# A planner's rules replaced by tables: the order on all engines of a gated mix of attention and feed-forward

## The chip, the cores and the metric

The kernel runs on one core of a Trainium2 chip. The metric is the device time of one execution in microseconds, as the median of several runs. The engines are named as the profile names them: PE (TensorE, the matmuls), DVE (VectorE), ACT (ScalarE), POOL (GpSimd) and SP (SyncE, which issues most DMAs).

## The reference

Two branches read the same x (2048 tokens, 512 features) and are mixed per token by a gate. Branch A is attention with a compressive memory: 32 heads of 16 features, four segments of 512 tokens, causal softmax inside a segment, plus a linear-attention read of the memory that earlier segments left. Branch B is a gated feed-forward with 1792 hidden features.

```python
for s in range(4):                                   # segments of 512 tokens
    logits = einsum('bhqd,bhkd->bhqk', qs, ks) * scale + mask
    a_dot = einsum('bhqk,bhkd->bhqd', softmax(logits), vs)
    a_mem = (phi(qs) @ M) / (phi(qs) @ z + 1e-06)
    o = sigmoid(beta) * a_mem + (1 - sigmoid(beta)) * a_dot
    M = M + phi(ks)^T vs;  z = z + sum(phi(ks))
a = concat(o) @ wo
b = (relu(x @ W_gate) * (x @ W_up)) @ W_down
out = g * a + (1 - g) * b            # g = sigmoid(sum(x * gate_w))
```

phi(t) is t + 1 for t > 0 and exp(t) otherwise. All inputs and the output are bfloat16.

## The kernel before

**The work.** For each segment s there are these kinds of work. `proj(s)`: q, k and v by dense matmuls of 128 x 128 on 512 columns (L791, L793), evacuated from PSUM by DVE or ACT (`qcp`, `kcp`, `vcp`), and two masked copies of k (`kmask`, L810 and L811). `att(s)`: the scores in 18 *visits* (`quad`, L913). A visit is a group of matmuls in row tiles of 32 that fills 2048 columns of PSUM, that is four banks; one exponential on ACT (`exp`, L929) turns them into E in SBUF, and POOL masks the diagonal blocks (`mask`, L935). `pv` (L969) multiplies E with V for eight heads at once in two banks, DVE transposes the result (L979) and a chain on DVE and POOL divides, scales and transposes it into oT. `mu` (L836) updates the memory and `num` (L856) reads it. `ffn(s)`: 14 blocks of gate and up matmuls (`wg`, `wu`, L1043), relu on DVE or ACT (L1052, L1051) and a product on DVE (`hm`, L1054). `outp(s)`: per 128 tokens one PSUM bank that sums the down projection (L1082) and the attention's output projection (L1075); DVE or ACT scales it (`fin`, L1091, L1092), and SP stores it. The last 128 tokens are done in a piece of 384 columns and one of 128.

**The start.** Eleven matmuls on constants (`warm`, L693) run while x and the weights land. Sixteen identity matmuls (`xt`, L707) transpose the first segment's x, which is loaded into hT; DVE and ACT copy the pieces to xT. The first q projection (`q0`) goes by quarters of the contraction, one matmul at a time, through four banks, then k, then v. Weights come in quarters (wq, wk, wv: 128 KB each) and in halves of quarters (wg, wu: 224 KB each), all issued by SP in the order wq, wk, wv, wg, wu. x of later segments, k for the memory update (`kT2`) and the memory's output (`aT`) are transposed by DMA, also from SP.

**The order.** Nothing is ordered by the text of the program. Each piece of work is an `Op` with its engines, a duration from a small cost model, and the buffers that it reads and writes. `program` puts the ops into queues with priorities, and `Sched.run` places them one by one: `_choose` takes, for the engine that is free first, the head of the queue that is ready and has the best priority, with random offsets from a list of seeds, one for every 8 us of planned time; `ready` holds back work whose reader is not due, `low` and `visit_in` keep banks free for the next visit, and `_bank_choice` picks PSUM banks. Where an op may run on two engines, the one that can start first gets it. From the placed order each engine's instruction list with its semaphore waits is written out (`_waits`, `emit`), so the chip sees a fixed order, and only waits decide when things run.

**Banks.** Visits always stand on banks 0 to 3:

```python
eps = [Epoch("main", 4, 0)] + [Epoch("side") for _ in range(4, nb)]
```

so a visit cannot start before the exponential of the visit before it is done. Banks 4 to 7 go round among the projections, the feed-forward, pv, mu, num and the output; these may also use low banks when no visit is near.

Of the kernel before, what the change touches and what calls it, by code (L numbers as in the profile page):

```python
# [2 lines left out]

# [6 lines left out]
ALU = mybir.AluOpType  # L10
# [4 lines left out]
LAT = 60.0  # L15
MU_G = 1
LAG = 0
PAIR = 1
LASTK = 17
HWAIT = 250.0  # L20
HEARLY = 3500.0
MWAIT = 500.0
PVR = 2
NEXT = 1150.0
TNN = 2
STRICT = 6000.0
PE_LAT = 175.0
SWITCH = 106.0
GATE_T = {0: 20000.0, 1: 44000.0, 2: 90000.0, 3: 140000.0}
UNIT_T = 400.0  # L30
X1_T = 19000.0
X2_T = 34000.0
H1_T = 14000.0
# [5 lines left out]
SBX = 0  # L39
LOW_T = {"main": 0.0, "att": 3000.0, "proj": 2000.0, "ffn": 2000.0, "mid": 3000.0, "out": 5000.0}  # L40
WIN = 8000.0
EVAC_P = 0.5
ND_P = 0.2
ADP = 1
TSP = 0
OAP = 0
UNITS = [[8] * 18] * 4
ORDER = [[(0, 1, 7, 2, 6, 3, 5, 4), (4, 0, 1, 7, 2, 6, 3, 5)] * 2] * 4
# [30 lines left out]
class Epoch:  # L79
    _n = 0  # L80

    def __init__(self, cls="mid", nb=1, at=None):
        self.nb = nb
        self.at = at
        self.group = (self,)
        Epoch._n += 1
        self.res = f"ACCep{Epoch._n}"
        self.bank = None
        self.readers = []
        self.cls = cls  # L90


class Op:
    __slots__ = ("engs", "eng", "fns", "occs", "lat", "reads", "writes", "name", "dma", "nbytes", "mode", "ep", "role",
                 "after", "nbk", "port", "base", "preds", "stream", "idx", "start", "end", "done", "cidx", "gate", "nd", "mates")

    def __init__(self, alts, reads=(), writes=(), name="", lat=0.0, dma=False, nbytes=0, mode="f", ep=None, role=None):
# [13 lines left out]
        self.after = 0.0  # L111
        self.nbk = 2
        self.port = name.startswith(PORT)
        self.base = None
        self.preds = []
        self.gate = None
        self.mates = ()
# [11 lines left out]
class Sched:  # L129
    ENGS = ("pe", "act", "dve", "pool", "sp")  # L130
    CAPS = {"ffn": 3, "proj": 2, "mid": 2, "out": 2}

    def __init__(self, ndma=16, nbanks=8, seeds=(0,)):
        self.seeds = seeds
        self.jit = {}
        self.knobs = {}
        self.low_from = False
        self.mates = ()
# [9 lines left out]
        self.queues = {e: [] for e in self.ENGS}  # L148
        self.dma_rr = 0
        self.port_free = 0.0  # L150
        self.relax = False
# [7 lines left out]
        self.busy = {e: 0.0 for e in self.ENGS}  # L159
        self.ops = []  # L160
        self.log = []
# [8 lines left out]
    def add(self, op):  # L170
# [42 lines left out]
        self.ops.append(op)  # L213
        return op

    def queue(self, prio, ops):
        by = {}
        for t in ops:
            for e in t.engs:
                by.setdefault(e, []).append(t)  # L220
        for e, ts in by.items():
            self.queues[e].append([prio, ts, 0])

    def _bank_free(self, prev, e):
        if prev is None:
            return 0.0
        return max((r.end + LAT for r in prev.readers if self.know[e][r.stream] < r.idx), default=0.0)

    def pv_due(self):
        q = self.queues["pe"][self.pvq]  # L230
        while q[2] < len(q[1]) and q[1][q[2]].done:
            q[2] += 1
        if q[2] >= len(q[1]) or q[1][q[2]].gate is None:
            return 0
        t = self.now["pe"] + 500.0
        return (PVR if q[1][q[2]].mates else q[1][q[2]].nbk) if all(p.done and p.end <= t for p, _ in q[1][q[2]].preds) else 0

    def next_visit(self):
        q = self.queues["pe"][self.attq]
        while q[2] < len(q[1]) and q[1][q[2]].done:  # L240
            q[2] += 1
        return q[1][q[2]] if q[2] < len(q[1]) else None

    def visit_in(self, dt):
        op = self.next_visit()
        if op is None:
            return False
        t = self.now["pe"] + dt
        if op.after > t or not all(p.done and p.end <= t for p, _ in op.preds):
            return False  # L250
        return all(p.done and p.end <= t + 700.0 for g in op.ep.group for rd in g.readers for p, _ in rd.preds if p.ep not in op.ep.group and p.cidx < op.cidx)

    def soon(self, dt):
        op = self.next_visit()
        if op is None or op.after - HEARLY > self.now["pe"] + dt:
            return False
        if not all(p.done and p.end + LAT <= self.now["pe"] + dt for p, _ in op.preds):
            return False
        t = max((self._bank_free(x, "pe") if x is None or all(r.done for r in x.readers) else 1e9) for x in self.bank_ep[:4])
        return t <= self.now["pe"] + dt  # L260

    def next_sides(self):
        op = self.next_visit()
        return 0 if op is None else len(op.ep.group) - 1

    def low(self, cls):
        return 0 if self.low_from and (self.relax or not self.visit_in(LOW_T[cls])) else 4

    def _bank_choice(self, ep, e, taken=()):
        cls, nb, n = ep.cls, ep.nb, len(self.bank_ep)  # L270
        idle = [i not in taken and (p is None or all(r.done for r in p.readers)) for i, p in enumerate(self.bank_ep)]
        if ep.at is not None:
            own = range(ep.at, ep.at + nb)
            return (ep.at, max(self._bank_free(self.bank_ep[i], e) for i in own)) if all(idle[i] for i in own) else None
        lo = 4 if cls == "side" else self.low(cls)
        if cls in ("proj", "ffn", "mid", "out"):
            held = sum(not f and p.cls == cls for f, p in zip(idle, self.bank_ep))
            if held + nb > (self.knob()[3] if cls == "ffn" else 2):
                return None
            free = sum(idle[lo:])  # L280
            if (free - nb < max(self.pv_due(), 1) if nb == 1 else free < (2 if self.relax else 3)):
                return None
            room = sum(idle[4:]) - (self.next_sides() if self.visit_in(self.knob()[1]) and not self.relax else 0)
        else:
            room = 8
        best = None
        for bi in range(lo, n - nb + 1):
            if not all(idle[bi:bi + nb]) or bi + nb > 4 and min(nb, bi + nb - 4) > room:
                continue
            ft = max(self._bank_free(p, e) for p in self.bank_ep[bi:bi + nb])  # L290
            key = ft + (300.0 if bi < 4 else 0.0)
            if nb == 1:
                key += 0.0 if not idle[bi ^ 1] else 200.0
            if best is None or key < best[2]:
                best = (bi, ft, key)
        return best and best[:2]

    def _banks(self, op, e):
        taken, out, t = set(), [], 0.0
        for ep in op.ep.group:  # L300
            bc = self._bank_choice(ep, e, taken)
            if bc is None:
                return None
            out.append((ep, bc[0]))
            taken |= set(range(bc[0], bc[0] + ep.nb))
            t = max(t, bc[1])
        return out, t

    def _pred_done(self, op, e):
        for p, war in op.preds:  # L310
            if war and not p.dma and p.eng == e and e == "pe" and p.done:
                continue
            yield p

    def ready(self, op, e):
        t0 = self.now[e]
        t = op.after - (HEARLY if op.mode == "r" and self.mode == "h" else 0.0)
        if op.gate is not None:
            if self.mode != "r" and not self.relax and not (op.gate.done and self.now["pe"] > op.gate.start + STRICT) and not (op.gate.done and (self.next_visit() is None or self.soon(NEXT))):
                return None  # L320
            for m in op.mates:
                for p in self._pred_done(m, e):
                    if p.eng != "pe":
                        if not p.done:
                            return None
                        t = max(t, p.end + LAT - 900.0)
            lo = self.low("att")
            ft = sorted(self._bank_free(p, e) for p in self.bank_ep[lo:] if p is None or all(r.done for r in p.readers))
            if len(ft) < op.nbk:
                return None  # L330
            t = max(t, ft[op.nbk - 1])
        for p in self._pred_done(op, e):
            if not p.done:
                return None
            if self.know[e][p.stream] < p.idx:
                t = max(t, p.end + LAT)
        if op.ep is not None:
            if op.role == "w" and op.ep.bank is None:
                for rd in [x for g in op.ep.group for x in g.readers]:
                    for p, _ in rd.preds:  # L340
                        if p.ep in op.ep.group or p.cidx > op.cidx:
                            continue
                        if not p.done:
                            return None
# [858 lines left out]
```

## Time and profile before

| | |
|---|---|
| runs, us | 265.08, 264.30, 264.28 |
| median, us | 264.3 |
| span of the profiled execution, us | 262.7 |
| between the span and the median, us | 1.6 |
| PE busy, us (share of the span) | 255.7 (97%) |
| ACT, DVE, POOL busy, us | 184.5, 179.1, 131.0 |
| granted PE clock | 1.00 |
| DMA, MB moved | 19.87 |

The page gives the span, from the first instruction to the last, and not the device time of the profiled execution itself; the median of the runs stands for that. A line of the page's groups names source line, engine, operation, and output and inputs, then the count, the busy time and the mean duration, and then how long the engine stood idle before and what ended that. A line of a timeline gives the start, the length and the group.

### The profile page before, as it was taken

How to read it: one execution, taken by the hardware profiler on the slowest of the kernel's cores; microseconds unless marked ns; L12 is line 12 of the kernel's file. 1: busy time of each engine (PE TensorE's matmuls, PEld its weight loads, DVE VectorE, ACT ScalarE, POOL GpSimd, SP SyncE). 2: the span in 40 equal slices, each digit the busy share in tenths (PEclk: the TensorE clock that was granted, in tenths of full speed). 3: DMA queues.
4: the chain of work that ended last, by engine and by line, in shares of the span. 5: the costliest groups of instructions: out<-in, count | busy, mean ns of one | idle time of the engine just before them, and what ended most of it. 6: DMA issues, size and time to landing. Idle time of an engine off the chain costs nothing.

```text
span 262.7 us, 6432 instructions
## 1 busy us (share of the span) xinstructions
PE 255.7 (97%) x2619; PEld 114.6 (44%) x2653; DVE 179.1 (68%) x356; ACT 184.5 (70%) x160; POOL 131.0 (50%) x295
## 2 busy tenths in 40 slices
PE   8999999999999999999999999999999999999996
PEld 5444443444443544334444544443444444344444
DVE  5488878789986587778788676757667716477600
ACT  4586689999789779785768787677777665676021
POOL 3036557564646466666555457836365354545100
PEclk9999999999999999999999999999999999999999
DMA  6989646930261134213040242010131101000011
GB/s 197 286 302 281 138 66 148 274 44 22 68 155 25 24 81 117 48 22 33 10 107 13 59 91 23 4 40 2 31 76 40 22 24 34 26 2 2 0 42 40
DMA packets 34925, 19.87 MB, mean 76 GB/s; under 512 B 24016, under 2 KB 34128, under 8 KB 34896
## 3 DMA queue, kind: packets, MB, share of 16 engines
q1 hardware_dynamic: 34800, 19.46, 30.4%
q8 instruction: 21, 0.34, 0.6%
q14 instruction: 8, 0.07, 0.1%
q10 hardware_dynamic: 96, 0.00, 0.0%
HBM read 10.40 MB, written 2.11 MB: 48 GB/s over the span
## 4 chain that ended last, share of the span: by engine, by line
PE 97%; issue 1%; DVE 1%
PE ps L1043 38%; PE ps L1082 19%; PE ps L793 11%; PE ps L913 9%; PE ps L969 6%; PE ps L791 5%; PE ps L1075 5%; PE ps L856 1%; PE ps L693 1%; PE ps L707 1%; PE ps L836 0%; DVE hT L1054 0%; DVE Tn L979 0%; DVE osb L746 0%; DVE osb L1091 0%
## 5 line engine op out<-in xcount | busy, mean ns | idle before, releaser
L935 POOL TENSOR_SCALAR_AFFINE_SELECT E<-E 64x256 bf16<-64x256 bf16 (+1 forms) x256 | 111.1, 445 | 111.9 <-ACT E L929 82.7
L929 ACT ACTIVATE E<-ps 128x2048 bf16<-128x2048 f32 x72 | 135.1, 1876 | 38.7 <-PE ps L913 38.6
L1043 PE MATMUL ps<-xT,wu 128*128 128x512 bf16 x213 | 57.2, 380 | 1.4 <-issue 1.3
L1043 PE MATMUL ps<-xT,wg 128*128 128x512 bf16 x219 | 57.7, 380 | 0.6 <-issue 0.3
L1082 PE MATMUL ps<-wd,hT 128*128 128x512 bf16 (+2 forms) x229 | 52.8, 367 | 0.9 <-issue 0.6
L1054 DVE TENSOR_TENSOR hT<-ps,rl 128x512 bf16<-128x512 f32 x56 | 38.5, 687 | 16.5 <-PE ps L1043 16.4
L1082 PEld LDWEIGHTS ps<-wd,hT 128*128 128x128 bf16 x238 | 21.4, 98 | 23.8 <-issue 2.4
L1043 PEld LDWEIGHTS ps<-xT,wg 128*128 128x128 bf16 x224 | 20.6, 98 | 25.7 <-issue 2.8
L1043 PEld LDWEIGHTS ps<-xT,wu 128*128 128x128 bf16 x224 | 20.1, 98 | 25.4 <-issue 3.5
L913 PE MATMUL ps<-qT,kp 32*128 32x192 bf16 (+7 forms) x512 | 28.6, 287 | 0.0
L979 DVE STREAM_TRANSPOSE Tn<-ps 128x512 f32<-128x512 f32 x32 | 21.3, 696 | 9.1 <-PE ps L969 9.1
L1052 DVE TENSOR_SCALAR rl<-ps 128x512 bf16<-128x512 f32 x30 | 20.7, 690 | 8.2 <-PE ps L1043 7.9
L1091 DVE TENSOR_SCALAR osb<-ps,omg 128x512 bf16<-128x512 f32 (+1 forms) x8 | 5.6, 700 | 26.0 <-PE ps L1082 15.1
L1051 ACT ACTIVATE rl<-ps 128x512 bf16<-128x512 f32 x26 | 15.5, 598 | 9.9 <-PE ps L1043 9.7
L913 PEld LDWEIGHTS ps<-qT,kp 32*128 32x128 bf16 x512 | 8.2, 92 | 25.3 <-issue 13.1
L969 PE MATMUL ps<-E,vaug 64*17 64x128 bf16 (+7 forms) x512 | 18.7, 283 | 0.0
L969 PE MATMUL ps<-E,vsh 64*17 64x128 bf16 (+7 forms) x512 | 18.3, 283 | 0.0
L1092 ACT ACTIVATE osb<-ps,omg 128x512 bf16<-128x512 f32 (+1 forms) x9 | 6.1, 675 | 16.4 <-PE ps L1075 14.0
L793 PE MATMUL ps<-xT,wq 128*128 128x512 bf16 x61 | 16.1, 391 | 0.4 <-issue 0.3
L1075 PE MATMUL ps<-wo,oT 128*128 128x512 bf16 (+2 forms) x67 | 16.2, 366 | 0.2 <-issue 0.2
L793 PE MATMUL ps<-xT,wk 128*128 128x512 bf16 x60 | 15.6, 380 | 0.4 <-issue 0.3
L791 PE MATMUL ps<-wv,xT 128*128 128x512 bf16 x63 | 15.3, 380 | 0.1
(68 smaller groups left out, 229.2 us busy)
## 6 DMA issues: line engine op xcount, KB each, us to landing
vsh<-vaug SPq DMA_DIRECT2D x8, 272.0 KB, 4.3
osb<-in_A_x_dram SPq DMA_DIRECT2D x16, 128.0 KB, 2.3
out_dram<-osb SPq DMA_DIRECT2D x15, 128.0 KB, 1.7
wg<-in_B_W_gate_dram SPq DMA_DIRECT2D x8, 224.0 KB, 5.0
wu<-in_B_W_up_dram SPq DMA_DIRECT2D x8, 224.0 KB, 5.9
wd<-in_B_W_down_dram SPq DMA_DIRECT2D x1, 1792.0 KB, 10.5
hT<-in_A_x_dram SPq DMA_DIRECT2D x2, 256.0 KB, 3.0
wq<-in_A_wq_dram SPq DMA_DIRECT2D x4, 128.0 KB, 3.3
```

Of the source, the lines that this page charges most:

```text
L791: ins = e.matmul(A(ep)[:, :], lhsT=V.xT[:, kt, tok + col * 128:tok + (col + 1) * 128], rhs=w[:, kt, :], start=(kt == 0), stop=(kt == KT - 1))
L793: ins = e.matmul(A(ep)[:, :], lhsT=w[:, kt, col * 128:(col + 1) * 128], rhs=V.xT[:, kt, tok:tok + 512], start=(kt == 0), stop=(kt == KT - 1))
L913: ins = q.matmul(dst, lhsT=V.kp[r, kslot(s, G), c, :], rhs=V.qT[r, qslot(s, G), q0:q0 + w], start=True, stop=True, tile_position=(32 * jj, ...
L929: acts.append(act(lambda a: a.activation(V.E[:, base * 512:base * 512 + min(2048, 4 * W)], PF[:, 0:min(2048, 4 * W)], ACT.Exp, scale=SCALE ...
L935: pools.append(pool(lambda g, ap=ap, lim=lim, pat=pat: g.affine_select(out=ap, in_=ap, compare_op=ALU.is_ge, fill=0.0, base=lim, pattern=[ ...
L969: ins = q.matmul(A(eps[p])[32 * jj:32 * jj + 17, 64 * (c + u):64 * (c + u + n)], lhsT=v[:, 8 * G + 2 * jj + p, :], rhs=V.E[r, f:f + 64 * n ...
L979: ds.append(dve(lambda e, p=p, ep=eps[p]: e.transpose(V.Tn[:, 2 * (G % (TNN // 2)) + p, :], A(ep)[:, :]), t_dve(512), writes=[f"Tn{2 * (G ...
L1043: ins = e.matmul(A(ep)[:, :], lhsT=w[:, kt, f * 128:(f + 1) * 128], rhs=V.xT[:, kt, c % XR * 512:(c % XR + 1) * 512], start=(kt == 0), sto ...
L1052: ("dve", lambda e, ep=eg, r=r: e.tensor_scalar(V.rl[:, r, :], A(ep)[:, :], 0.0, None, ALU.max), t_dve(512))],
L1054: evs.append(dve(lambda e, ep=eu, r=r, hs=hs: e.tensor_tensor(V.hT[:, hs, :], A(ep)[:, :], V.rl[:, r, :], ALU.mult), t_dve(512), reads=[f" ...
L1075: ins = e.matmul(A(ep)[:, 0:c1 - c0], lhsT=V.oT[:, ot[G], i * 128:(i + 1) * 128], rhs=V.wo[:, G, c0:c1], start=st_ and G == 0, stop=sp_ an ...
L1082: ins = e.matmul(A(ep)[:, 0:c1 - c0], lhsT=V.hT[:, slots[f], i * 128:(i + 1) * 128], rhs=V.wd[:, f, c0:c1], start=st_ and f == f0, stop=sp ...
```

## The change

The queues, the priorities, the seeds and the rules of choice go. In their place stand two tables. `ORDER` lists, for each of the five engines, the numbers of the ops in the order in which the engine runs them; an op that may run on two engines runs on the one whose list names it. `BANKS` gives one digit, the first PSUM bank, for each use of PSUM in the order in which the program names them. `run` places the ops by these lists. The cost model stays, but it now only decides how the lists are merged, which DMA semaphore a load gets and in what order waits are written.

A visit is no longer tied to banks 0 to 3: it is one use of four banks, whose first bank comes from `BANKS`, and the exponential reads from there. PSUM banks are no longer cleared at the start, and the first matmuls no longer wait for that. The four first banks are no longer a buffer of their own: warm-up, xt and the first k columns take banks by the table. The first matmul of an output tile no longer waits for all of hT, but only for what it reads. The order of the loads on SP and of the three small loads on ACT (`touch`) comes from the tables as well.

```diff
+SPLIT = {2: (2,), 4: (4,), 5: (4, 1), 6: (4, 2)}
+BANKS = ("130453107213460547754000000570000447000004700055766574475646577645465476647467556655640576747455500000450000656000104500"
...
+ORDER = {k: [int(x) for x in v.split()] for k, v in {
+    "pe": """
+57 58 59 63 61 65 69 67 73 71 168 133 169 143 134 148 138 149 139 163 158 135 164 136 170 144 145 173 146 171 174 183 195 189 184 159 160 190 384 385
...
+    "sp": """
+0 1 2 3 7 6 8 9 4 11 15 5 21 17 13 10 12 16 14 26 18 85 37 23 19 83 156 20 22 36 38 24 182 81 25 181 199 200 39 30 27 157 29 45 87 28 42 31 40 43 92
...
+    def start_of(self, op, e):
+        t = 0.0
+        for p in self._preds(op, e):
             if not p.done:
                 return None
+            t = max(t, p.end + LAT)
+        if op.ep is not None and op.role == "w":
+            for p in self._holders(op):
+                for r in p.readers:
+                    if not r.done:
+                        return None
+                    t = max(t, r.end + LAT)
...
     def run(self):
+        for ep in self.eps:
+            if ep.at is None:
+                ep.bank = int(self.banks[ep.idx])
...
+        todo = {e: [self.ops[i] for i in self.order[e]] for e in self.ENGS}
...
         while True:
+            heads = [(e, todo[e][at[e]]) for e in self.ENGS if at[e] < len(todo[e])]
+            if not heads:
+                return
+            cands = [(t, self.ENGS.index(e), e, op) for e, op in heads for t in (self.start_of(op, e),) if t is not None]
...
             start, _, e, op = min(cands, key=lambda c: c[:2])
             self.place(op, e, start)
-            self.relax = False
+            at[e] += 1
...
-            k["reads"] = list(k.get("reads", ())) + [f"init{i}" for i in range(4)]
...
-    for b in range(4):
-        ds.append(dve(lambda e, b=b: e.memset(PS[:, 4 + b, :], 0.0), 500, writes=[f"init{b}"], name=f"init{b}"))
...
-            eps = [Epoch("main", 4, 0)] + [Epoch("side") for _ in range(4, nb)]
+            eps, part = [], []
+            for n in SPLIT[nb]:
+                part += [(len(eps), j) for j in range(n)]
+                eps.append(Epoch("main", n))
...
+                    return a.activation(V.E[:, base * 512 + c0:base * 512 + c0 + n], PF[:, x.bank * 512:x.bank * 512 + n], ACT.Exp, scale=SCALE)
...
-                        rd = [f"oT{ot[G]}" for G in range(4)] + ["wo"] + ([] if last else ["wd"] + [f"hT{x}" for x in slots])
+                        rd = [f"oT{ot[G]}" for G in range(4)] + ["wo"]
...
-                        rd = [f"hT{slots[f]}" for f in ((f0, f0 + 1) if not st_ else range(NF - 4))]
+                        rd = [f"hT{slots[f]}" for f in (f0, f0 + 1)]
```

In the list for SP, numbers 0 and 1 are x, 2 to 5 the quarters of wq, 6 to 9 those of wk, 10 to 13 those of wv, 14 to 21 the first halves of wg and wu, 22 and 23 two small vectors, and 24 to 31 the second halves of wg and wu; 36 to 39 transpose x of the second segment, and 156 is the first transpose of k.

654 lines of the change are left out of this document (154 added, 500 removed), and 36 rows, old and new, of the table ORDER.

## The prediction

> **What bounds the kernel now.** I read the page's busy times and its chain first, then the waits of TensorE, then its timeline by stretches, then both ends of the span.
>
> ```profile
> PE 255.7 (97%) x2619; PEld 114.6 (44%) x2653; DVE 179.1 (68%) x356; ACT 184.5 (70%) x160; POOL 131.0 (50%) x295
> ...
> PE 97%; issue 1%; DVE 1%
> ```
>
> TensorE is busy for 255.7 of 262.7 us, and the chain that ended last runs on it for 97%. The other engines have 30% to 50% to spare. Busy shares can hide short waits, so the second view is TensorE's own waits:
>
> ```profile
> PE ps L1043 <- issue: 1.6, 10, 0.2
> PE ps L693 <- PEq L1188: 0.8, 1, 0.8
> ...
> PE ps L1043 <- DVE Tn L979: 0.2, 1, 0.2
> ```
>
> Apart from the 0.8 us of start-up, no wait is longer than 0.2 us. Where a matmul's record is missing, an idle time of about one matmul appears, so even these may be none. The timeline decides it, since a stream without waits has a fixed pitch:
>
> ```profile
> 20.29 1.03 PE L1043 MATMUL ps<-xT,wu 128*128 128x512 bf16 x4
> 21.15 1.03 PE L1043 MATMUL ps<-xT,wg 128*128 128x512 bf16 x4
> 22.11 0.40 PE L913 MATMUL ps<-qT,kp 32*128 32x320 bf16 x8
> 22.44 1.04 PE L1043 MATMUL ps<-xT,wu 128*128 128x512 bf16 x4
> ...
> 30.22 1.03 PE L1043 MATMUL ps<-xT,wu 128*128 128x512 bf16 x4
> 31.18 0.39 PE L969 MATMUL ps<-E,vaug 64*17 64x512 bf16 x4
> ...
> 32.28 0.40 PE L913 MATMUL ps<-qT,kp 32*128 32x448 bf16 x8
> 32.61 0.70 PE L836 MATMUL ps<-vaug,phik 128*64 128x68 bf16 x32
> ...
> 34.11 1.03 PE L1043 MATMUL ps<-xT,wu 128*128 128x512 bf16 x4
> ...
> 87.11 0.42 PE L856 MATMUL ps<-Mbd,phiq 128*128 128x136 bf16 x4
> 87.36 1.89 PE L1082 MATMUL ps<-wd,hT 128*128 128x512 bf16 x8
> ...
> 256.37 2.44 PE L1082 MATMUL ps<-wd,hT 128*128 128x384 bf16 x14
> ...
> 259.29 0.94 PE L1082 MATMUL ps<-wd,hT 128*128 128x128 bf16 x14
> ```
>
> Columns are start, length, instructions. Four dense matmuls take 21.15 - 20.29 = 0.86 us, or 0.216 each. A score visit begins 0.10 us after the dense stream would have gone on (21.15 + 0.86 = 22.01, start 22.11) and takes 22.44 - 22.11 = 0.33. The weighted sums of V (pv, L969) begin at 31.18, again 0.10 after 30.22 + 0.86, and end where the next visit starts: 1.10. That visit takes 0.33 to 32.61 without another 0.10, since it follows pv directly. The memory update (mu) runs from 32.61 to 34.11 less four dense matmuls (one block of four lies between): 0.64. A num group takes 0.25. By (length - last one's 0.33 or 0.22) / 13 the 384-wide matmuls have a pitch of 0.16 and the 128-wide ones of 0.06.
>
> The start:
>
> ```profile
> 0.84 2.93 PE L693 MATMUL ps<-const-bfloat16-1.0 128*128 128x512 bf16 x11 [0.84 <-PEq L1188]
> 3.69 1.95 PE L707 MATMUL ps<-ident,hT 128*128 128x128 bf16 x16
> 5.43 4.21 PE L793 MATMUL ps<-xT,wq 128*128 128x512 bf16 x16
> 9.48 3.19 PE L793 MATMUL ps<-xT,wk 128*128 128x512 bf16 x13
> 12.60 0.40 PE L913 MATMUL ps<-qT,kp 32*128 32x512 bf16 x4
> ...
> L793 PE MATMUL ps<-xT,wq x16: 379/379/634, 5.4 to 9.3; 128*128 128x512 bf16 x16
> ```
>
> Sixteen q matmuls take 9.48 - 5.43 = 4.05 us instead of 16 x 0.216 = 3.46; the last row (shortest, median and longest duration) shows some of 0.63 us among many of 0.38. The excess of 0.6 us is three slow ones at about 0.43, 0.43 and 0.39.
>
> Now the whole stream by count. Both builds have 946 dense matmuls from the first q on: 910 of width 512, 18 of 384, 18 of 128. So 1.24 + 907 x 0.216 + 18 x 0.16 + 18 x 0.06 = 201.1. To that 72 visits x 0.33 = 23.8, 16 pv x 1.10 = 17.6, three mu x 0.64 = 1.9, twelve num x 0.25 = 3.0, and 73 changes from the dense stream into these kinds x 0.10 = 7.3: 254.7 in all. 5.43 + 254.7 = 260.1.
>
> ```profile
> 260.07 0.39 PE L1075 MATMUL ps<-wo,oT 128*128 128x128 bf16 x4
> 260.10 1.11 SPq L1094 DMA_DIRECT2D out_dram<-osb  x2
> 260.50 0.35 DVE L1091 TENSOR_SCALAR osb<-ps,omg 128x128 bf16<-128x128 f32 x1 [10.86 <-PE ps L1075]
> ```
>
> TensorE's last four start at 260.07, three pitches before 260.3. So all its waits between 5.43 and the end come to about 0.2 us. What follows is a scaling on DVE, a store and its landing, up to 262.7. The median of the runs, 264.3, is 1.6 us above this span, and I keep that distance. The runs spread over 0.8 us (264.28 to 265.08); 0.3%, or 0.8 us, is about what a measurement can tell from no change.
>
> **The change, part by part.**
>
> *Order on TensorE.* I counted the same things in the changed build: 448 gate and up matmuls, 192 of q, k and v, 306 of the output projections, 72 visits, 16 pv, three mu, twelve num, and again 73 changes of kind. Visits and pv that follow each other directly are as many as before. So the stream is 254.7 us long as well: 0. A table can shorten this kernel only by waits, and 0.2 us of waits are there to remove.
>
> *Visits on any four banks.* Of 72 visits, 71 stand on banks 0 to 3 and one on 1 to 4. Every visit still waits for the exponential of the one before it:
>
> ```profile
> L929 ACT ACTIVATE E<-ps 128x2048 bf16<-128x2048 f32 x72 | 135.1, 1876 | 38.7 <-PE ps L913 38.6
> ...
> L811 ACT ACTIVATE kp<-kT,pm 128x512 bf16<-128x512 bf16 x7 | 5.0, 719 | 0.0
> ...
> L1092 ACT ACTIVATE osb<-ps,omg 128x512 bf16<-128x512 f32 (+1 forms) x9 | 6.1, 675 | 16.4 <-PE ps L1075 14.0
> ```
>
> A visit's 0.33 and 1.88 of exponential make 2.2 us; the shortest distance from visit to visit is ten dense matmuls and a visit, 2.16 + 0.33 = 2.5 us, three times in the old order and once in the new one. The old ones show no wait, so the new one should not: 0 (bounds 0 and 0.2).
>
> *Evacuating engines.* relu stays at 30 on DVE and 26 on ACT. Seven more masks of k go to ACT (14 for 7) and five final scalings leave it (4 for 9): 7 x 0.72 - 5 x 0.68 = +1.6 us on an engine with 78 us to spare. On the path only if ACT is late for a visit: 0. If that cover fails somewhere, one mask ahead of an exponential costs 0.7.
>
> *What is dropped.* Four PSUM memsets on DVE and the waits for them lie under the landing of x: 0. The tail keeps its last pieces, 384 and 128 wide, and their store; the 384 scaling moves from ACT to DVE, 18 x 0.06 = 1 us before DVE is needed for the 128: 0.
>
> *Order of loads.* Here the new table can lose. SP's queue puts two quarters of wq behind wk, and gate and up weights among wq and wv.
>
> ```profile
> 0.81 0.87 SPq L619 DMA_DIRECT2D hT<-in_A_x_dram  x2
> 7.42 1.85 SPq L619 DMA_DIRECT2D wg<-in_B_W_gate_dram  x4
> 17.59 1.21 SPq L621 DMA_TRANSPOSE xT<-in_A_x_dram  x1
> 20.59 1.30 SPq L816 DMA_TRANSPOSE phik<-ek  x1
> ...
> wg<-in_B_W_gate_dram SPq DMA_DIRECT2D x2, 224.0 KB, 4.4
> ...
> wg<-in_B_W_gate_dram SPq DMA_DIRECT2D x8, 224.0 KB, 5.0
> wu<-in_B_W_up_dram SPq DMA_DIRECT2D x8, 224.0 KB, 5.9
> wq<-in_A_wq_dram SPq DMA_DIRECT2D x4, 128.0 KB, 3.3
> ...
> wv<-in_A_wv_dram SPq DMA_DIRECT2D x4, 128.0 KB, 3.8
> ```
>
> The fifteenth load is issued at 7.42, so loads are (7.42 - 0.81) / 14 = 0.47 us apart. wq's third quarter is now ninth: 0.81 + 8 x 0.47 + 3.3 = 7.9, needed at the 17th matmul, 9.5: covered. wv's first quarter is sixteenth, issued at 7.9. It is needed by the 30th matmul, which starts at 5.43 + 1.24 + 26 x 0.216 = 12.3. With 3.8 us (wv today) it lands at 11.7; with 5.0 (median of all wg) at 12.9; with 4.4 (the two wg issued around 7.9) at 12.3. More large loads than today lie ahead of it, so I take 12.5: a wait of +0.2 (bounds 0 and +0.6). Behind it in TensorE's queue stand the rest of v and the first visit; all of it shifts by that much, and later loads gain the same slack.
>
> *Small loads on ACT.* Three of 1 KB leave the first two microseconds and are issued later from ACT, between exponentials. How long TensorE waits for x at the start is in the view of its tile:
>
> ```profile
>   DMA hT<-in_A_x_dram: 0.2, 1
> ```
>
> If x landed sooner without the small loads, at most this 0.2 us goes: bounds -0.2 and 0, and I take -0.1. [...]
>
> Sum: 264.3 + 0 + 0.2 - 0.1 = 264.4 us.
>
> **The rivals.**
>
> *The loads come too late* (slower). The first up block of the feed-forward (L1043, f = 0) needs the third quarter of wu for the second half of its contraction. That load is now 28th, behind two transposes that hold SP's queue for 1.2 and 1.3 us. It is issued at about 0.81 + 25 x 0.47 + 2.5 = 15.1; at today's 5.9 us it lands at 21.0. TensorE gets there after 60 dense matmuls and three visits: 5.43 + 1.24 + 57 x 0.216 + 3 x 0.43 = 20.3. That is a wait of 0.7, or 0.9 if SP is held a little longer: 265.1 to 265.3. Against it: 5.9 us is the time of loads issued one on another, and transposes thin the queue; with 4.4 us it lands at 19.5 and costs nothing. It decides from about 5.2 us on. Chance 0.13.
>
> *The clock opens sooner* (faster). The slow stretch of 16 identity matmuls (5.43 - 3.69 = 1.74 us) and three q matmuls (1.24) halves where TensorE is at full rate earlier. [...] The order that leads up to it is the same in both kernels, so this would be luck of a run and not the change, and a median takes most of it away. Chance 0.07. [...]
>
> *A mid-run wait* (slower): one mask of k on ACT just ahead of an exponential that frees the banks of the next visit, 0.7 each, twice or more to be seen: 265.8. No place stands out by count. Chance 0.05.
>
> **How the numbers follow.** Forecast, within 0.3%: 0.75; its own range 263.9 to 264.9. Faster by over 0.3%: 0.07, the clock alone. Slower: 0.13 + 0.05 = 0.18. Eight in ten lie between 263.7, which gives away most of the clock's case, and 265.2, which takes in most of the late loads.
>
> **What would show it.** After the change: TensorE busy about 256 us, dense blocks of four 0.86 apart, visits at 0.43, the first q at 5.4, the last TensorE group about 260 to 260.4. A wait on wv near 12.3 or on wu near 20.3 in TensorE's timeline is the price I gave the loads. I am wrong if TensorE's stream is shorter than 254.7 us, or if waits of more than 0.8 us stand in it anywhere else.

## The result, and the profile after

The changed kernel takes 265.06 us (median of six runs, 264.93 to 265.14) and the kernel before 264.29 us (264.17 to 265.08). The ratio is 1.0029, interval 1.0016 to 1.0043. A second measurement, among the experiments below, gave 265.23 against 264.15 us: 1.0034, interval 1.0023 to 1.0045. So the change costs 0.3%, just at the bound that the prediction drew between "the same" and "slower": the first measurement lies below it and the second above.

The page of the changed kernel, its busy times and its chain of waits:

```profile
PE 254.9 (97%) x2617; PEld 113.9 (43%) x2653; DVE 176.7 (67%) x350; ACT 185.6 (71%) x162; POOL 121.3 (46%) x295
...
PE 93%; DVE 2%; issue 2%; DMA 2%
```

Before, the chain was TensorE for 97%. Now DVE and a DMA have 2% each. TensorE's own waits name the place (us in total, times, longest):

```profile
PE ps L502 <- PEq L888: 0.8, 1, 0.8
PE ps L800 <- DVE Mc L620: 0.5, 1, 0.5
```

The first line is the start-up of before. The second is new. The chain of waits around it (start, length, what) shows how it came about:

```profile
31.09 4.27 DMA osb<-in_A_x_dram
35.36 0.02 issue
35.38 0.93 DVE osb L537
36.31 0.01 DVE gl L537
36.32 0.27 DVE eb L522
36.59 0.30 DVE Mc L620
36.89 0.05 issue
36.94 0.60 PE ps L800 x2
37.54 0.86 PE ps L576 x4
38.41 0.86 PE ps L800 x4
...
41.00 0.33 PE ps L689 x4
```

SP issues a row block of x (`ldxr3`) at 31.09, and it lands 4.27 us later. DVE's list has the gate's reduction over it (`gate3`, L537) ahead of the addition to the memory (`mum0`, L620), which frees a bank of PSUM. TensorE's timeline there:

```profile
36.00 0.40 PE L689 MATMUL ps<-qT,kp 32*128 32x320 bf16 x8
36.94 0.60 PE L800 MATMUL ps<-xT,wu 128*128 128x512 bf16 x2 [0.54 <-DVE Mc L620]
```

Its next block should start at 36.33, 0.33 after its visit at 36.00. It starts at 36.94, 0.61 late. The two rows of 0.86 and the visit of 0.33 show the pitch of before: outside its stops the stream is what it was.

The start of the changed kernel, TensorE's timeline (start, length, group):

```profile
3.67 1.67 PE L511 MATMUL ps<-ident,hT 128*128 128x128 bf16 x16
5.31 1.25 PE L576 MATMUL ps<-xT,wq 128*128 128x512 bf16 x5
6.54 2.47 PE L576 MATMUL ps<-xT,wk 128*128 128x512 bf16 x10
8.84 0.59 PE L576 MATMUL ps<-xT,wq 128*128 128x512 bf16 x2
...
12.39 0.39 PE L689 MATMUL ps<-qT,kp 32*128 32x512 bf16 x4
```

The view of the tile wq has the durations of the q matmuls (shortest, median and longest, in ns):

```profile
L576 PE MATMUL ps<-xT,wq x60: 379/379/390, 5.3 to 131.2; 128*128 128x512 bf16 x60
```

Before, some q matmuls took 634 ns. Here none takes over 390: the clock's record in the trace opens at 4.86 us of the span, and at 6.63 in the profile of before. Yet not much is gained. Five q matmuls should end at 5.31 + 5 x 0.216 = 6.39, and k begins at 6.54, a stop of 0.15; ten of k should end at 8.70, and q goes on at 8.84, a stop of 0.14. The view of the tile wk has what its instructions, weight loads into TensorE and matmuls together, waited for (us in total, times); the weight loads overlap the matmuls (113.9 and 254.9 us busy in a span of 263.0), so this total is more than the two stops:

```profile
  DMA wk<-in_A_wk_dram: 0.9, 2
```

At its first visit the kernel is 12.60 - 12.39 = 0.21 us ahead of before, and in the new order one matmul more stands ahead of that visit, so 0.43 us by equal work. The stop at 36.3 takes it away.

The tail is as forecast:

```profile
260.33 0.39 PE L830 MATMUL ps<-wo,oT 128*128 128x128 bf16 x4
260.50 0.96 SPq L848 DMA_DIRECT2D out_dram<-osb  x2
260.75 0.35 DVE L845 TENSOR_SCALAR osb<-ps,omg 128x128 bf16<-128x128 f32 x1 [0.28 <-PE ps L830]
```

The span grew from 262.7 to 263.0, which is 0.3 of the 0.8 us. The rest is not in a comparison of these two profiles, for two reasons. First, the profiled execution of before was not a typical one: its span is 262.7, and the median span of 25 runs of before on one chip and of 35 on another is 262.4. Second, the time that lies outside the span differs between the kernels. In 98 runs of before it is 1.68 to 1.80 us, mean 1.73; in 18 of the changed kernel 2.00 to 2.10, mean 2.05. So in the second measurement the 1.08 us between the medians are 0.75 of span (263.15 against 262.4) and 0.31 outside it.

### The profile page after: what moved, and what is told of

The parts are those of the page before. It is cut to its first block, busy times and chain, and to the rows that moved or that the text cites. A ratio compares the mean times of both kernels' runs of the same rounds, so it can differ in the third digit from the quotient of the medians.

```text
span 263.0 us, 6393 instructions
## 1 busy us (share of the span) xinstructions
PE 254.9 (97%) x2617; PEld 113.9 (43%) x2653; DVE 176.7 (67%) x350; ACT 185.6 (71%) x162; POOL 121.3 (46%) x295
## 4 chain that ended last, share of the span: by engine, by line
PE 93%; DVE 2%; issue 2%; DMA 2%
PE ps L800 36%; PE ps L837 19%; PE ps L576 10%; PE ps L689 8%; PE ps L738 6%; PE ps L574 5%; PE ps L830 5%; DMA osb<-in_A_x_dram 2%; PE ps L632 1%; PE ps L502 1%; PE ps L511 1%; PE ps L615 0%; DVE osb L537 0%; DVE hT L811 0%; DVE Mc L620 0%
## 5 line engine op out<-in xcount | busy, mean ns | idle before, releaser
L708 POOL TENSOR_SCALAR_AFFINE_SELECT E<-E 64x256 bf16<-64x256 bf16 (+1 forms) x256 | 101.2, 422 | 100.3 <-ACT E L700 89.5
L800 PE MATMUL ps<-xT,wu 128*128 128x512 bf16 x217 | 60.1, 380 | 1.5 <-issue 0.6
L837 PE MATMUL ps<-wd,hT 128*128 128x512 bf16 (+2 forms) x227 | 56.4, 366 | 1.2 <-issue 1.0
L800 PEld LDWEIGHTS ps<-xT,wg 128*128 128x128 bf16 x224 | 20.8, 98 | 25.8 <-issue 1.9
L689 PE MATMUL ps<-qT,kp 32*128 32x384 bf16 (+7 forms) x512 | 28.6, 287 | 0.0
L755 POOL TENSOR_TENSOR adT<-Tn,rdg 128x512 bf16<-128x512 f32 x12 | 12.9, 1074 | 14.7 <-DVE rdg L753 14.6
L845 DVE TENSOR_SCALAR osb<-ps,omg 128x512 bf16<-128x512 f32 (+2 forms) x13 | 9.2, 710 | 14.6 <-PE ps L830 8.8
L576 PE MATMUL ps<-xT,wk 128*128 128x512 bf16 x63 | 17.7, 380 | 0.1
L576 PE MATMUL ps<-xT,wq 128*128 128x512 bf16 x60 | 17.4, 380 | 0.4 <-issue 0.3
L574 PE MATMUL ps<-wv,xT 128*128 128x512 bf16 x62 | 16.7, 380 | 0.3 <-issue 0.2
```

The lines of the kernel that those rows point to most:

```text
L574: ins = e.matmul(A(ep)[:, :], lhsT=V.xT[:, kt, tok + col * 128:tok + (col + 1) * 128], rhs=w[:, kt, :], start=(kt == 0), stop=(kt == KT - 1))
L576: ins = e.matmul(A(ep)[:, :], lhsT=w[:, kt, col * 128:(col + 1) * 128], rhs=V.xT[:, kt, tok:tok + 512], start=(kt == 0), stop=(kt == KT - 1))
L689: ins = q.matmul(dst, lhsT=V.kp[r, kslot(s, G), c, :], rhs=V.qT[r, qslot(s, G), q0:q0 + w], start=True, stop=True, tile_position=(32 * jj, ...
L708: pool(lambda g, ap=ap, lim=lim, pat=pat: g.affine_select(out=ap, in_=ap, compare_op=ALU.is_ge, fill=0.0, base=lim, pattern=[[0, 4]] + pat ...
L800: ins = e.matmul(A(ep)[:, :], lhsT=w[:, kt, f * 128:(f + 1) * 128], rhs=V.xT[:, kt, c % XR * 512:(c % XR + 1) * 512], start=(kt == 0), sto ...
L837: ins = e.matmul(A(ep)[:, 0:c1 - c0], lhsT=V.hT[:, slots[f], i * 128:(i + 1) * 128], rhs=V.wd[:, f, c0:c1], start=st_ and f == f0, stop=sp ...
```

## The experiments

All twelve kernels ran with a profile and were timed beside the kernel before on the same chip. The table gives the medians; "span against before" is the median span less that of the runs of before beside it.

| kernel | time, us | before, us | ratio, interval | span against before, us | outside the span, us |
|---|---|---|---|---|---|
| before_again | 264.30 | 264.10 | 1.0008 (0.9996 to 1.0021) | +0.15 | 1.74 |
| after_again | 265.23 | 264.15 | 1.0034 (1.0023 to 1.0045) | +0.75 | 2.04 |
| gate3_later | 265.01 | 264.10 | 1.0032 (1.0020 to 1.0045) | +0.60 | 2.04 |
| x3_earlier | 264.94 | 264.10 | 1.0036 (1.0019 to 1.0052) | +0.55 | 2.03 |
| x3_later | 266.47 | 264.10 | 1.0085 (1.0066 to 1.0105) | +2.10 | 2.00 |
| qkv_first | 265.10 | 264.15 | 1.0029 (1.0017 to 1.0041) | +0.70 | 2.02 |
| qkv_gate | 265.19 | 264.15 | 1.0033 (1.0020 to 1.0045) | +0.80 | 2.02 |
| qkv_gate_touch | 264.81 | 264.15 | 1.0021 (1.0010 to 1.0033) | +0.45 | 1.92 |
| loads_gate | 265.89 | 264.43 | 1.0060 (1.0039 to 1.0081) | +1.05 | 2.17 |
| q_before_k | 265.54 | 264.43 | 1.0048 (1.0031 to 1.0064) | +0.65 | 2.17 |
| q_k_braw | 264.84 | 264.25 | 1.0025 (1.0012 to 1.0039) | +0.20 | 2.16 |
| q_k_braw_touch | 264.60 | 264.25 | 1.0011 (1.0000 to 1.0023) | +0.10 | 2.03 |

The before_again row shows what such a difference is worth: the same kernel against itself gives +0.15.

The diffs below are pieces of the lists in `ORDER`. The numbers that matter: on SP 2 to 5 are the quarters of wq, 6 to 9 of wk, 10 to 13 of wv, 14 to 17 of the first wg, 18 to 21 of the first wu; 23 is beta, 87 is `ldxr3`; 33 to 35 are ACT's small loads and 32 is the operation (L474) that the expectations call its table load, whose own record stands at 0.80 us for 1.28 us in the changed kernel and at 0.81 for 1.28 in before; 88 is `gate3`, 259 `mum0`.

**First theory: the stop at 36.3.** It was tested from both sides and by making it larger.

gate3_later, DVE's list:

```diff
-88 77 259 326 334 86 336
+77 259 326 334 88 86 336
```

> The changed kernel with one operation moved: on DVE the gate reduction of x row 3 stands behind reb, mum0, qcp1_0 and qcp1_1 and no longer ahead of them. Theory (DVE's list puts an operation that waits for a load ahead of the addition that frees TensorE's bank): the hole of 0.61 us on TensorE at 36.3 goes, span 263.0 - 0.6 = 262.4, time 265.06 - 0.6 = 264.45. Rival (the 0.8 us lie at the start or outside the profiled span, and the hole is caught up later): time within 0.15 us of 265.06.

x3_earlier, SP's list:

```diff
-39 30 27 157 29 45 87 28 42 31
+39 30 87 27 157 29 45 28 42 31
```

> The changed kernel with the load of x row 3 issued four places earlier on SP (near 27.5 us and not 31.1). Theory: it lands by 32 us, before DVE asks for it at 33.8, so the hole on TensorE at 36.3 goes without any move on DVE: 264.45 us, as with the reduction moved. Rival (the hole comes from DVE being busy with the reduction itself, 0.93 us, ahead of the addition, not from the load): of the 0.61 at most a part goes, since the reduction still stands ahead of the addition; time 264.7 or above.

x3_later, SP's list:

```diff
-45 87 28 42 31
+45 28 42 87 31
```

> The changed kernel with the load of x row 3 issued behind one more weight load and one transpose on SP, at about 33.5 us and not 31.1. Theory: every 0.1 us that the load lands later is 0.1 us more of a hole on TensorE at 36.3. With the 4.3 us it took it would land 2.4 us later (time 267.4), with 2.3 us, the median of these loads, 0.4 us later (265.5). Rival (the hole is caught up later): 265.06 as before.

before_again is the kernel before, unchanged:

> The kernel before, unchanged, with another profile. Theory (the profiled execution of before was a slow one, its clock opening 1.8 us late at 6.6 us of the span): some executions show a first q near 5.3 and a span of 262.2 at a time of 264.3, so that the distance from span to time is 2.05 us in both kernels. Rival (the distance differs between the kernels, 1.6 and 2.05 us): spans of 262.7 at 264.3 again.

The stop is real as a mechanism. In x3_later TensorE's waits show it with another size:

```profile
PE ps L800 <- DVE Mc L620: 1.5, 1, 1.5
```

and the chain of waits where it comes from:

```profile
33.77 3.17 DMA osb<-in_A_x_dram
...
38.28 0.61 PE ps L800 x2
```

The load is issued 2.7 us later and lands 1.6 us later than in the profile of the changed kernel, and the span is 1.5 us longer than that of gate3_later. In gate3_later and x3_earlier there is no stop at 36, and still their spans are those of the changed kernel: 263.0 and 262.95. Theory and expectation (264.45) fall. Only the lowest spans moved: 262.6 in both, against 262.9 in the 18 runs of the changed kernel, twelve of them on another chip. The profiles, one of each kernel, say where the 0.6 us went: all three kernels were later at the start. TensorE's timeline of gate3_later:

```profile
5.73 1.24 PE L576 MATMUL ps<-xT,wq 128*128 128x512 bf16 x5 [0.54 <-DMA wq<-in_A_wq_dram]
```

and of x3_earlier:

```profile
9.21 0.59 PE L576 MATMUL ps<-xT,wk 128*128 128x512 bf16 x2
10.12 1.04 PE L576 MATMUL ps<-xT,wq 128*128 128x512 bf16 x4 [0.32 <-DMA wq<-in_A_wq_dram]
```

and the chain of waits of x3_later:

```profile
5.99 4.04 DMA wq<-in_A_wq_dram
10.02 0.05 issue
10.07 2.33 PE ps L576 x10
```

In x3_earlier two matmuls from 9.21 should end at 9.64, and the next starts 0.48 late; in x3_later the stop is 0.57 long. In both of these it is wq's fourth quarter, the twelfth load, that is waited for. The first visit begins at 12.73, 12.86 and 12.77 us in them, and not at 12.39. before_again settled the other question: it has a first q at 5.43, a span of 262.8 and a distance of 1.74, so the distance is a property of the kernel and the rival held.

**Second theory: the loads at the start.** Four kernels on one chip, the first of them the changed kernel as it is.

> The changed kernel, unchanged, beside the three below. What the first runs left open: with the hole at 36.3 taken out, the median span stayed at 263.0 us, since the first score visit began at 12.7 to 12.9 us and not at 12.4. Theory (the hole stands in every run, and the start has a floor of its own, set by loads): spans of 262.9 to 263.6, median 263.3, time 265.3, with a distance from span to time of 2.03 us. Rival (the hole is an accident of the first profile): spans as with the reduction moved, 262.6 to 263.3, median 263.0.

Its profile has no stop at 36.3 at all, and a span of 262.9. It has a stop for wk instead, in TensorE's timeline:

```profile
6.42 1.04 PE L576 MATMUL ps<-xT,wk 128*128 128x512 bf16 x4
7.83 1.47 PE L576 MATMUL ps<-xT,wk 128*128 128x512 bf16 x6 [0.37 <-DMA wk<-in_A_wk_dram]
```

The chain of waits has its load:

```profile
4.08 3.70 DMA wk<-in_A_wk_dram
```

Four matmuls of k from 6.42 should end at 7.28. The next starts at 7.83, 0.55 late, when wk's fourth quarter has landed at 7.78. The first visit begins at 12.72, and at 36.8 TensorE comes when the addition on DVE is just done. So a TensorE that is early at 12 us is stopped at 36, and one that is late at 12 us is not: the stop of the first profile and the waits for wk and wq are floors of the same stream, and taking one away leaves the next. This is read from single profiles; how often an execution of the changed kernel has the one start or the other is not known.

qkv_first, SP's list:

```diff
-2 3 7 6 8 9 4 11 15 5 21 17 13 10 12 16 14 26 18
+2 3 7 6 8 9 4 5 11 10 13 12 15 21 17 16 14 26 18
```

> The changed kernel with SP's first loads in another order: all quarters of wq, wk and wv ahead of those of the gate and up weights (wq's fourth quarter is tenth and not twelfth, wv's first two eleventh and twelfth and not sixteenth and tenth). Theory (the order of loads sets a floor under the start: in three of four profiles of the new order TensorE stands still for 0.2 to 0.6 us near 9.4 to 10.1 until wq's fourth quarter has landed, at 9.6 to 10.1 us, so that an early opening of the clock is worth nothing): no stop there, the first score visit at 11.8 to 12.7 us as the clock falls, span 0.4 to 0.6 us below the changed kernel's. Rival (the start varies with the clock alone, and the loads only fill time that is lost anyway): the same span within 0.15 us.

Its first visit is the earliest of these, 12.28 us. But the gate and up weights are now behind, and this is the wait that the prediction had as a rival, on the third quarter of wu. The chain of waits:

```profile
15.36 5.07 DMA wu<-in_B_W_up_dram
```

and TensorE's timeline:

```profile
19.58 0.59 PE L800 MATMUL ps<-xT,wu 128*128 128x512 bf16 x2
20.47 1.04 PE L800 MATMUL ps<-xT,wu 128*128 128x512 bf16 x4 [0.30 <-DMA wu<-in_B_W_up_dram]
```

The two matmuls from 19.58 should end at 20.01, so the next is 0.46 late. Before it, at 14.60, TensorE stood for 0.26 us until a quarter of wg had landed at 14.55. The span is that of after_again within 0.05 us: gained early, lost later.

qkv_gate is qkv_first with the edit of gate3_later:

> The changed kernel with both edits: loads of wq, wk and wv first, and the gate reduction of x row 3 behind the four operations on DVE. Theory: both gains add up, 0.5 from the start and 0.6 from the hole: median span 262.2, time 264.2, which is the time of before; the distance from span to time stays at 2.03. Rival (what is gained early is lost later at another wait): time 264.7 or above.

Nothing adds up: 263.2. Its start had a first q at 5.72 and a stop for wk until 7.96, and its first visit came at 12.82.

qkv_gate_touch, ACT's list on top of that:

```diff
-62 70 64 74 32 140
+32 33 34 35 62 70 64 74 140
...
-406 33 226 418 237 34 35 243
+406 226 418 237 243
```

> As the one before it, with ACT's table load and its three 1 KB loads back at the head of ACT's list, ahead of the copies of x. Theory (they set what lies outside the profiled span: 1.73 us in every run of before, 2.03 in every run of the new order): the distance falls to 1.73 and the time by 0.3, to 263.9. Rival (the distance comes from something else in the program): it stays at 2.03; by the prediction's own term x would land up to 0.2 us later, so time 264.2 to 264.4.

The distance fell by 0.10 and not by 0.3, from 2.02 to 1.92, and the time by 0.38; the span, 0.35 lower, has no reason in the profile (a first visit at 12.63, with the wait for wk still there).

**Third theory: TensorE's own list asks for k too early.** In the new list k begins with the sixth matmul after x, in the old one with the seventeenth. Two kernels on another chip. Both have gate3_later's edit and SP's first loads in sequence; q_before_k also has TensorE's start with q first, and DVE's and ACT's first copies in that order.

```diff
-2 3 7 6 8 9 4 11 15 5 21 17 13 10 12 16 14 26 18 85 37 23 19 83 156 20 22
+2 3 4 5 6 7 8 9 10 11 12 13 14 15 16 17 18 19 20 21 26 85 37 23 83 156 22
```

> The changed kernel with SP's first 22 loads in the order of before (wq, wk, wv, first gate and up weights, each with its quarters in sequence) and the gate reduction of x row 3 behind the four operations on DVE; TensorE's list stays as changed, with k from its sixth matmul on. So wk's fourth quarter is tenth and not eighth, and the third quarter of wu 21st and not 28th. Theory (the start is set by what TensorE's new list asks for and when that load lands): it stands for wk near 7 us until 8.2 to 8.5, 0.4 to 0.6 longer than before the edit, and does not stand at 20 us; first score visit 13.0 to 13.4, span 263.3 to 263.6. Rival (the order of loads alone, without TensorE's, makes up the loss): span 262.4 as before.

```diff
-168 133 169 143 134 148 138 149 139 163 158 135 164 136 170 144 145 173 146 171 174 183 195
+168 133 143 158 169 134 144 135 170 145 136 146 171 138 139 148 149 163 164 173 174 183 195
...
-62 70 64 74 32 140 153 165 147 175 196
+62 70 64 74 32 147 140 165 153 175 196
...
-60 66 68 72 150 154 56 137 142 141 172 155 176
+60 66 68 72 56 137 172 150 142 141 154 155 176
```

> As loads_gate, and TensorE's list at the start put back to q before k: thirteen matmuls of q, then those of k, with ACT's and DVE's first copies out of PSUM in the same order; all else as in the changed kernel. Theory (TensorE's new list asks for k 3 us earlier than the old one, ahead of the loads, so that an early opening of the clock is worth nothing, and later the third quarter of wu and x row 3 hold it once more): no stop of over 0.1 us from the first q to 37 us, first score visit at 11.8 to 12.7 as the clock falls, median span 262.4 as before, and with the distance of 2.03 a time of 264.4. Rival (the loss lies elsewhere in the start): span 263.0, time 265.0.

loads_gate did what the theory said, and more (TensorE's waits):

```profile
PE ps L576 <- DMA wk<-in_A_wk_dram: 1.1, 1, 1.1
```

With the loads of before under the new list of TensorE the first visit comes at 13.51 us and the time is 265.89. So the two lists belong together: under TensorE's new order the loads of before cost more than the new ones. The fourth pairing, TensorE's old order with the new loads, was not run.

q_before_k has no wait for a weight, and a first visit at 12.37. It lost most of it again at one place that neither theory named. TensorE's waits:

```profile
PE ps L689 <- ACT E L700: 0.5, 1, 0.5
```

TensorE's timeline around it:

```profile
19.41 1.46 PE L800 MATMUL ps<-xT,wu 128*128 128x512 bf16 x6
21.38 0.40 PE L689 MATMUL ps<-qT,kp 32*128 32x320 bf16 x8 [0.51 <-ACT E L700]
```

ACT's timeline:

```profile
19.33 0.23 ACT L520 ACTIVATE eb<-braw 128x32 f32<-128x32 bf16 x1 [1.61 <-DMA braw<-in_A_beta_dram]
19.46 1.86 ACT L700 ACTIVATE E<-ps 128x2048 bf16<-128x2048 f32 x1
```

And the chain of waits:

```profile
13.60 5.71 DMA braw<-in_A_beta_dram
```

8 KB of beta were issued at 13.60, 1.1 us later than in the changed kernel, and landed 5.71 us after that, where the changed kernel shows 3.60. In both kernels a transpose is issued just ahead of them; what q_before_k has more is two weight loads ahead of them. ACT's list has the operation on beta ahead of the exponential that frees the next visit's banks. The six matmuls from 19.41 should end at 20.71 and the fourth visit should start 0.10 later, at 20.81; it starts at 21.38, 0.57 late. The 0.68 of the next expectation counts that 0.10 in.

The last two kernels take that away. q_k_braw, SP's list against q_before_k:

```diff
-20 21 26 85 37 23 83 156
+20 21 23 26 85 37 83 156
```

> As q_before_k, with the load of 8 KB for the gate's beta three places earlier on SP, ahead of a transpose. What the run before this showed: the start had no stop for a load, but beta landed at 19.3 us, and ACT's list has the operation that waits for it ahead of the exponential that frees the banks of the fourth visit: TensorE stood 0.68 us at 20.5. Theory (beta's load was the last of these stops, and TensorE's place at the end is the sum of its stops): beta lands near 14 to 17 us, no stop at 20.5, median span 263.35 - 0.6 = 262.7, which is that of before on the same chip within 0.3. Rival (another load or operation takes its place): span 263.0 or above, with a stop of 0.3 us or more between 12 and 37 us.

> As q_k_braw, with ACT's table load and three 1 KB loads back at the head of ACT's list. Theory (their place on ACT sets part of what lies outside the profiled span: with them at the head it was 1.92 and not 2.02 us on one chip): 0.1 less outside the span, start unchanged, time 0.1 below q_k_braw. Rival (the prediction's term: without them x lands sooner): the first matmul of q up to 0.2 us later, time the same or up to 0.2 above.

In the view of TensorE's waits q_k_braw has the start-up of 0.8 us alone. Its timeline:

```profile
5.17 2.98 PE L576 MATMUL ps<-xT,wq 128*128 128x512 bf16 x13
7.98 3.90 PE L576 MATMUL ps<-xT,wk 128*128 128x512 bf16 x16
11.72 0.59 PE L574 MATMUL ps<-wv,xT 128*128 128x512 bf16 x2
12.24 0.39 PE L689 MATMUL ps<-qT,kp 32*128 32x512 bf16 x4
...
259.74 0.39 PE L830 MATMUL ps<-wo,oT 128*128 128x128 bf16 x4
```

From the first q to 37 us no stop of over 0.2 us is left (the longest is 0.18 at 8.59, when a quarter of wk has landed at 8.54), the last group starts at 259.74 and not at 260.33, and the median span is 262.7: 0.65 below q_before_k, as expected, and 0.20 above before. With the small loads back at ACT's head it is 262.6, and the distance 2.03 and not 2.16. So the loss inside the span is accounted for to within 0.1 to 0.2 us, about what before_again shows as the error. It is the order of the first 37 us, all engines' lists together; q_before_k against loads_gate shows that under the loads of before TensorE's order, with the copies that follow it, is worth 13.51 - 12.37 = 1.14 us at the first visit, but no run shows how the loss of the changed kernel itself divides between TensorE's list and that of the loads. What q_k_braw keeps of the changed kernel, the tables of the remaining 220 us and the free banks of the visits, gains nothing and costs little: from the first visit to the last group it takes 259.74 - 12.24 = 247.50 us and q_k_braw_touch 247.33, where before takes 247.47, or 247.25 for equal work (one matmul less).

The 0.3 us outside the span are not settled. The small loads on ACT are worth 0.10 and 0.13 of it (two pairs of kernels). With SP's first loads in sequence it was about 0.13 longer (2.00 to 2.04 in the six kernels without that have the small loads late, on two chips; 2.16 to 2.17 in three on a third chip; before has 1.73 to 1.74 on all three). The span holds every instruction that the profile records, so the profile can't show what happens there.

No version beats the kernel before: the best, q_k_braw_touch, is at 1.0011 (1.0000 to 1.0023).

## Why the prediction was right, and where it was not

The forecast was 264.4, between 263.7 and 265.2, with 0.75 on "within 0.3%". The time came out at 265.06: inside these bounds, outside the 263.9 to 264.9 that the forecast gave for its main case, and in the class as forecast, though at its edge (1.0029, and 1.0034 in the second measurement). The steps behind it were only partly right.

That the number held is in part luck. In the profile of the changed kernel TensorE stands for 0.15 + 0.14 + 0.61 = 0.90 us, none of it at the two places that the prediction named for a late load; by its own sign, waits of more than 0.8 us anywhere else, it was wrong there. Against this the first q came at 5.31 and not 5.43, and the 0.60 us of slow q matmuls fell away, together 0.72 us, through an early clock that the forecast had left to a rival with a chance of 0.07. The last group is then 260.33 - 260.07 = 0.26 late, and the other 0.3 us of the time lie outside the span, where the sum carried over the distance of before.

*TensorE's stream by count.* Right. Blocks of four take 0.86 us and visits 0.33 as before, the last group starts at 260.33 where 260 to 260.4 was forecast, and after 41 us there is no stop of over 0.2 us. That the order of the tables brings nothing, since no waits are left to remove, held.

*Order on TensorE: 0.* Wrong at the start, and this is the step that failed. The count was taken of how many matmuls there are, and not of which weight each of the first thirty asks for. The new list asks for k 3 us earlier (at 6.4 instead of 9.5), which gives stops of 0.14 to 0.55 us for wk and of 0.48 and 0.57 for wq's fourth quarter in the profiles of the changed kernel and of its variants with one edit; put back together with its loads, and with the two small stops on DVE and ACT taken out, q first leaves 0.20 of the 0.75 us of span.

*Order of loads: +0.2.* The size was that of one stop, the place was wrong. It was priced on wv's first quarter at 12.3 us; in no profile does a first matmul on wv start more than 0.03 us late for a load. The quarters that were checked, wq's third and wv's first, are not those that bind. And the times by which loads are needed were read from one execution whose clock opened late, at 6.63 us. In the twelve profiles of the changed list and its variants it opened at 3.48 to 5.70, and then loads are needed sooner: 0.57 us at the first visit (12.24 in q_k_braw against 12.60 with one matmul less ahead of it). A load that is covered in the late execution need not be in an early one.

*Small loads off ACT's head: -0.1.* Wrong in sign, and no run shows the term. In its place the runs showed this: x's second half landed at 4.35 us of the span and at 4.34 before, by the semaphores' record in the trace, so x gained nothing; over all profiles it landed at 3.97 to 4.35 in the ten without these loads at ACT's head and at 4.11 to 4.34 in the four with them. And with them there the time fell by 0.38 (qkv_gate_touch) and 0.24 (q_k_braw_touch). Of this 0.10 and 0.13 are outside the span; the rest, inside it, has no cause in the profiles. These landings show no price of three loads of 1 KB beside two of 256 KB.

*The distance of 1.6 us from span to median.* Wrong. It joined the median of the runs to the span of an execution that was 0.3 us longer than the median one, and it was carried over to a kernel where it is 2.05 us.

*The rival "loads come too late".* Its place, the third quarter of wu near 20.3, had no stop in the changed kernel's first profile and one of 0.09 in its second; in the first the load, issued at 15.36 us, had landed by 19.71. In qkv_first it was issued at 15.36 too, took 5.07 us, and stopped TensorE at 20.01 for 0.46 us: for this start it decides from 20.01 - 15.36 = 4.65 us on, and not from the 5.2 of the prediction. The mechanism was right and three other loads carried it: wk, wq's fourth quarter, and the row of x at 36 us. Since they are floors of one stream, their prices don't add; in the range they stand as one case, as priced.

*The rival "clock opens sooner".* It did open sooner, by 6.63 - 4.86 = 1.8 us. No run of before shows it open ahead of 6.63 us (6.79 in its second profile), so the lower bound of 263.7, drawn for this case, was the author's estimate and is shown by no run. The halving is shown: until the clock opens, the q matmuls of before start 0.43 us apart and the identity matmuls 0.107, in the first profiles of both kernels; after it q goes at 0.216 and, in the changed kernel, the identity matmuls at 0.056. By this rule, half of the slow work, 1.8 us would be worth 0.9; the first visit shows 0.43 by equal work, which is the 0.72 us above less the stops of 0.15 and 0.14 for wk. That the moment comes by luck alone, as the prediction had it, these runs neither show nor exclude: the profiles of before opened at 6.63 and 6.79 us, all twelve of the new lists before 5.71. In the first profile of before this is 6.63 - 0.84 = 5.79 us after the first matmul, in that of the changed kernel 4.86 - 0.84 = 4.02; what sets the moment was not shown.

*The mid-run wait.* The kind was right (an engine's list that puts an operation with a late input ahead of one that frees banks), the engine and the input were others: DVE and a row of x at 36.3, 0.61 us, and, in a variant only, ACT and beta at 20.8, 0.57 us.

## What to carry to other kernels

When an order is changed, check for each of the first operations which load it needs and when that load lands, and do so for the earliest opening of the clock seen and not for the one execution on record (in the fourteen profiles here it opened at 3.48 to 6.79 us). Loads that come just in time make a row of floors: removing one stop alone gave 0.2 us at most here and removing all of them 0.55 to 0.65, so test the whole start at once. In a fixed list, an operation that waits for a DMA should not stand ahead of one that frees a bank, however small its data: 8 KB of beta cost TensorE 0.57 us at 20.8 us, 128 KB of x 0.61 at 36.3.

## What was not expected of the hardware

The time outside the profiled span is a property of the kernel that two measurements give alike to within 0.03 us: 1.73 us in before, 2.06 and 2.04 in the changed kernel, 1.92 to 2.17 in the variants. Between variants the order of loads at the start moves it by 0.10 to 0.13; why before has 0.3 less is open.

The 8 KB of beta took 3.60 us to land in the changed kernel, 4.31 in loads_gate, 5.71 in q_before_k with the same list on SP, 5.58 in q_k_braw without a transpose just ahead, and 6.40 in before. So neither their size nor the transpose sets it alone, and what does was not tested. 128 KB of x, in the middle of the run, took 4.27 us where the median of such loads is 2.6 us.

The runs of the changed kernel spread less than those of before: 0.2 against 0.9 us in the first measurement, 0.6 against 1.7 in the second. That floors set by loads hide the variation of the start would explain it, but is not shown: no trace of before's shortest runs (span 261.8 to 262.0) exists to show what they did at the start.
